# Four layers interleaved by superblocks in shared pools, with score tiles of 3 and 2 banks

## The chip, the core and the metric

The kernel runs on one core of a Trainium2 chip. The metric is the device time of one execution in microseconds (us). "Span" is the length of the one profiled execution; it is 1.7 to 2.8 us under the time of that same run.

Engines: PE is TensorE (matmul), PEld its weight loads, DVE is VectorE, ACT is ScalarE, POOL is GpSimd, SP is SyncE. PSUM is the memory that PE writes its results to; the kernel uses it in 8 banks of 512 float32 columns per row. Work is cut into four superblocks of 512 tokens, numbered 0 to 3.

## The reference

Four layers run one after the other, A B A B, each `x = x + layer(layernorm(x))` on a 2048 x 512 bfloat16 x. A is attention with a sliding window of 256 and 32 heads of 16. B is linear attention.

```python
def _A_ref(x, wqkv, wo):          # q, k, v = x @ wqkv, 32 heads of 16
    scores = jnp.einsum("bhqd,bhkd->bhqk", q, k) * (Dh ** -0.5)
    mask = (idx[:, None] - idx[None, :] >= 0) & (idx[:, None] - idx[None, :] < 256)
    p = _softmax(jnp.where(mask[None, None], scores, -1e9), axis=-1)
    return merge_heads(jnp.einsum("bhqk,bhkd->bhqd", p, v)) @ wo

def _B_ref(x, wqkv, wo):
    phi = lambda t: jnp.where(t > 0, t + 1, jnp.exp(t)) + 1e-6
    pq, pk = phi(q), phi(k)
    kv = jnp.einsum("bhsd,bhse->bhde", pk, v)      # a sum over ALL positions
    z = jnp.einsum("bhsd->bhd", pk)
    num = jnp.einsum("bhqd,bhde->bhqe", pq, kv)
    den = jnp.einsum("bhqd,bhd->bhq", pq, z)[..., None] + 1e-6
    return merge_heads(num / den) @ wo
```

(Head merging is abbreviated.) One dependence matters throughout. B's K, V and Q of a superblock can start once A's output of that superblock is there. B's output can start only after the K and V of all four superblocks.

## The kernel before

Each layer is a function with its own pools, and a layer ends before the next begins. In attention, score tiles are two buffers of 3 PSUM banks, and everything else shares 2 banks. Layer B has all 8 banks to itself (6 + 2 for K, V and Q, then 4 + 4 for the output).

```python
# layer A: scores of 3 head pairs x 2 runs into one 3-bank tile, exp, masks on POOL, PV later
psA = ctx_l.enter_context(tc.tile_pool(name="psA", bufs=2, space=PSUM))
psM = ctx_l.enter_context(tc.tile_pool(name="psM", bufs=2, space=PSUM))
...
A = psA.tile([P, 3, 2, 4, 64], F32, name="A", tag="psA")
...                                   # score matmuls: 32 rows, 64 to 256 columns
nc.scalar.activation(body[:, 0:2 * ng, 0:n, :], A[...], ACT.Exp, scale=0.25)
...                                   # affine_select on POOL for the diagonal blocks
# PV: lhsT = two 64-key blocks of probabilities, rhs = 34 columns of V
nc.tensor.matmul(O[:, u, g, :, :], lhsT=PTs[b][:, s0:s0 + 2, :], rhs=vbd[...], ...)
...
# layer B, first half: 6 + 2 banks of its own
psP1 = ctx_p1.enter_context(tc.tile_pool(name="psP1", bufs=6, space=PSUM))
psKV = ctx_p1.enter_context(tc.tile_pool(name="psKV", bufs=1, space=PSUM))
...
nc.scalar.copy(vs[:, :, 0:P], pv[:].rearrange("p (t c) -> p t c", t=NCT))   # V copy on ACT
...
# the V of layer A is staged in vst (3 buffers) and spread into vbd by four small DMAs per tile
st = vst[vst_n[0] % 3]
```

Of the kernel before, what the change touches and what calls it, by code (L numbers as in the profile page):

```python
# [8 lines left out]
ACT = mybir.ActivationFunctionType  # L9
# [22 lines left out]
R1 = [(7, 7, 1), (-2, 0, 3)]  # L32
R2 = [(5, 5, 3), (-4, 0, 1)]
R3 = [(1, 1, 3), (0, 4, 1)]
R4 = [(3, 3, 3), (2, 6, 1)]
R5 = [(0, 0, 4)]
R6 = [(2, 2, 4)]
R7 = [(-1, 0, 4)]
R8 = [(4, 4, 4)]
R9 = [(-3, 0, 2), (6, 6, 2)]  # L40
R10 = [(1, 4, 2), (3, 6, 2)]
BINS = [(R3, R4), (R5, R6), (R1, R2), (R7, R8), (R9, R10)]
BINS0 = [(R3, R4), (R5, R6), (R8, R10), ([(5, 5, 3)], [(7, 7, 1), (6, 6, 2)])]
GROUPS = [(0, 1, 2), (3, 4, 5), (6, 7, 8), (9, 10, 11), (12, 13), (14, 15)]


def bin_windows(bins):

    win = {u: [] for u in range(4)}
    for b, runs in enumerate(bins):  # L50
        for r, run in enumerate(runs):
            pos = 0
            for (j, w0, n) in run:
                w = w0
                if w % 2:
                    assert pos == 0
                    win[w // 2].append((b, r, -1, j))
                    w += 1
                while w + 1 < w0 + n:
                    win[w // 2].append((b, r, pos + w - w0, j))  # L60
                    w += 2
                if w < w0 + n:
                    assert pos + w - w0 == 3
                    win[w // 2].append((b, r, pos + w - w0, j))
                pos += n
    return win


def bin_masks(runs):

    found = {}
    for r, run in enumerate(runs):
        pos = 0
        for (j, w0, n) in run:
            for w in range(w0, w0 + n):
                if w - j in (0, 4):
                    found.setdefault((w - j, pos + w - w0), []).append(r)
            pos += n
    return [(k, pos, rs) for (k, pos), rs in sorted(found.items())]
# [3 lines left out]
def build(ctx, tc, A_x, A_wqkv, A_wo, B_x, B_wqkv, B_wo, out, layers="ABAB", force_safe=False):  # L83
    nc = tc.nc
    S = A_x.shape[-2]
    NT, NSS = S // P, S // 512

# [3 lines left out]
    small = ctx.enter_context(tc.tile_pool(name="small", bufs=6))  # L91
    work = ctx.enter_context(tc.tile_pool(name="work", bufs=3))
# [4 lines left out]
                            base=0, pattern=[[-1, P]], channel_multiplier=1)  # L97
    pidx = consts.tile([P, 1], I32, name="pidx")
# [3 lines left out]
    mask_odd = consts.tile([P, 1], F32, name="mask_odd")  # L102
    nc.vector.tensor_copy(mask_odd[:], par_i[:])
    mask_even = consts.tile([P, 1], F32, name="mask_even")
    nc.vector.tensor_scalar(mask_even[:], mask_odd[:], -1.0, 1.0, op0=ALU.mult, op1=ALU.add)
    mhalf = consts.tile([P, 1], F32, name="mhalf")
    nc.vector.memset(mhalf[:], -0.5)
# [3 lines left out]
    nc.gpsimd.memset(bd[:], 1.0)  # L111
    nc.gpsimd.affine_select(out=bd[:], in_=bd[:], compare_op=ALU.is_ge, fill=0.0,
                            base=0, pattern=[[-16, 8], [0, 16]], channel_multiplier=1)
    nc.gpsimd.affine_select(out=bd[:], in_=bd[:], compare_op=ALU.is_ge, fill=0.0,
                            base=15, pattern=[[16, 8], [0, 16]], channel_multiplier=-1)
    nA = layers.count("A")
    vflags = consts.tile([1, max(nA, 1)], F32, name="vflags")
    nc.vector.memset(vflags[:], 1.0)

    wA = wpool.tile([P, NCT, 3 * D], BF, name="wA")  # L120
# [550 lines left out]
```

## Time and profile before

The median was 607.03 us (604.7 to 607.84, four runs beside those of the changed kernel). The trace is of another execution, of 602.24 us.

| stage | length, us | PE busy | ACT busy |
|---|---|---|---|
| start, to the first exp of attention | 41.1 | | |
| attention of layer 1 | 170.1 | 83% | 84% |
| middle (layer B and what surrounds it) | 115.5 | 77% | 32% |
| attention of layer 3 | 170.4 | 83% | 84% |
| tail (last layer B) | 103.1 | 75% | 28% |

### The profile page before, as it was taken

How to read it: one execution, taken by the hardware profiler on the slowest of the kernel's cores; microseconds unless marked ns; L12 is line 12 of the kernel's file. 1: busy time of each engine (PE TensorE's matmuls, PEld its weight loads, DVE VectorE, ACT ScalarE, POOL GpSimd, SP SyncE). 2: the span in 40 equal slices, each digit the busy share in tenths (PEclk: the TensorE clock that was granted, in tenths of full speed). 3: DMA queues.
4: the chain of work that ended last, by engine and by line, in shares of the span. 5: the costliest groups of instructions: out<-in, count | busy, mean ns of one | idle time of the engine just before them, and what ended most of it. 6: DMA issues, size and time to landing. Idle time of an engine off the chain costs nothing. (4 is left out here: it accounts for less than half of the span.)

```text
span 600.2 us, 15126 instructions
## 1 busy us (share of the span) xinstructions
PE 460.0 (77%) x6032; PEld 250.1 (42%) x6114; DVE 332.5 (55%) x729; ACT 367.5 (61%) x373; POOL 272.1 (45%) x667
## 2 busy tenths in 40 slices
PE   0178888888878879995647788888887887899573
PEld 0133455545546534452213345554544553444231
DVE  7731546545623365777886154554562336677773
ACT  1557679799779824660025857988978892466000
POOL 9444457657556562200035435675755666320000
PEclk9996899999976678997988779899998788999787
DMA  9412115031020030211431211501302103021363
GB/s 302 127 27 60 16 37 75 2 48 30 2 64 11 3 80 10 41 31 35 72 70 36 57 19 34 78 2 42 35 2 53 24 2 76 14 44 29 74 120 92
DMA packets 83375, 29.66 MB, mean 49 GB/s; under 512 B 67936, under 2 KB 82784, under 8 KB 83296
## 3 DMA queue, kind: packets, MB, share of 16 engines
q1 hardware_dynamic: 78256, 23.88, 19.9%
q10 hardware_dynamic: 5040, 4.72, 2.6%
q8 instruction: 50, 0.82, 0.6%
q14 instruction: 29, 0.24, 0.1%
HBM read 6.29 MB, written 2.10 MB: 14 GB/s over the span
## 5 line engine op out<-in xcount | busy, mean ns | idle before, releaser
L298 ACT ACTIVATE pt<-A 128x1536 bf16<-128x1536 f32 (+1 forms) x228 | 281.0, 1321 | 52.9 <-PE A L286 46.3
L308 POOL TENSOR_SCALAR_AFFINE_SELECT pt<-pt 128x384 bf16<-128x384 bf16 (+3 forms) x456 | 184.3, 430 | 140.1 <-ACT pt L298 136.1
L318 PE MATMUL O<-vbd,pt 128*128 128x34 bf16 x2880 | 108.4, 182 | 27.7 <-POOL pt L308 22.7
L318 PEld LDWEIGHTS <-pt 128*128 128x128 bf16 x2880 | 89.8, 99 | 64.8 <-POOL pt L308 37.9
L286 PE MATMUL A<-qT,kb 32*128 32x192 bf16 (+3 forms) x1920 | 96.7, 249 | 17.1 <-ACT pt L298 14.6
L286 PEld LDWEIGHTS <-kb 32*128 32x128 bf16 x1920 | 50.1, 98 | 69.6 <-issue 64.3
L490 PE MATMUL py<-woB,oT 128*128 128x512 bf16 x124 | 39.3, 448 | 16.6 <-DMA oT<-ob 14.1
L327 DVE RECIPROCAL rall<-O 128x24 f32<-128x24 f32 (+1 forms) x48 | 13.8, 288 | 66.7 <-PE O L318 66.7
L164 POOL TENSOR_SCALAR ln_ve<-ln_mv 128x1 f32<-128x1 f32 x64 | 14.0, 225 | 69.7 <-DVE ln_mv L162 68.2
L221 PE MATMUL pq<-xnT,wA 128*128 128x512 bf16 x108 | 37.3, 432 | 9.2 <-DVE ln_stats L160 5.6
L271 PE MATMUL py<-woA,oT 128*128 128x512 bf16 x108 | 33.1, 397 | 14.1 <-DMA oT<-o_sb 12.4
L160 DVE BATCH_NORM_STATS2 ln_stats<-xres 128x6 f32<-128x512 f32 x64 | 42.5, 681 | 0.8
L235 DVE TENSOR_SCALAR kb<-pk,mask_even 128x512 bf16<-128x512 f32 x32 | 25.3, 791 | 28.6 <-PE pk L232 24.4
L232 PE MATMUL pk<-xnT,wA 128*128 128x512 bf16 x116 | 36.5, 414 | 5.0 <-ACT kb L237 2.5
L403 ACT ACTIVATE phi_e<-pkb 128x512 bf16<-128x512 f32 x32 | 19.1, 598 | 32.9 <-PE pkb L426 31.4
L166 POOL TENSOR_TENSOR ln_rstd<-ln_ve,mhalf 128x1 f32<-128x1 f32 x64 | 36.8, 582 | 4.3 <-ACT xn L178 0.4
L226 DVE CAST qT<-pq 128x512 bf16<-128x512 f32 x24 | 16.6, 691 | 33.5 <-PE pq L221 33.4
L432 PE MATMUL pvb<-wB,xnTb 128*128 128x512 bf16 x124 | 34.8, 395 | 0.2
L426 PE MATMUL pkb<-wB,xnTb 128*128 128x512 bf16 x122 | 34.0, 396 | 0.5 <-issue 0.4
L272 DVE TENSOR_TENSOR xres<-py,xres 128x512 f32<-128x512 f32 x32 | 22.0, 686 | 21.4 <-PE py L271 20.5
L245 PE MATMUL pv<-wA,xnT 128*128 128x512 bf16 x114 | 31.9, 380 | 2.2 <-ACT kb L237 0.8
L178 ACT ACTIVATE xn<-xres,ln_nmr,ln_rstd 128x512 bf16<-128x512 f32 x12 | 9.6, 827 | 37.9 <-DVE ln_nmr L176 37.9
(71 smaller groups left out, 522.0 us busy)
## 6 DMA issues: line engine op xcount, KB each, us to landing
vbd<-vst SPq DMA_DIRECT2D x128, 34.0 KB, 1.9
out_dram<-ost ACTq DMA_DIRECT2D x16, 128.0 KB, 1.9
wB<-in_B_wqkv_dram SPq DMA_DIRECT2D x1, 1536.0 KB, 11.2
xst<-in_A_x_dram SPq DMA_DIRECT2D x8, 128.0 KB, 2.6
wA<-in_A_wqkv_dram SPq DMA_DIRECT2D x2, 512.0 KB, 7.2
xst<-in_A_x_dram ACTq DMA_DIRECT2D x8, 128.0 KB, 4.0
wA<-in_A_wqkv_dram ACTq DMA_DIRECT2D x1, 512.0 KB, 4.3
woA<-in_A_wo_dram ACTq DMA_DIRECT2D x1, 512.0 KB, 8.2
```

Source lines behind the costliest of these rows:

```text
L160: nc.vector.bn_stats(stats[:], x_ap)
L166: nc.gpsimd.tensor_tensor(rstd[:], ve[:], mhalf[:], op=ALU.pow)
L221: nc.tensor.matmul(pq[:], lhsT=w[:, c, t * P:(t + 1) * P], rhs=xnTs[I][:, c, :], start=(c == 0), stop=(c == NCT - 1))
L232: nc.tensor.matmul(pk[:], lhsT=w[:, c, D + t * P:D + (t + 1) * P], rhs=xnTs[I][:, c, :], start=(c == 0), stop=(c == NCT - 1))
L271: nc.tensor.matmul(py[:], lhsT=oT[:, c, :], rhs=wo[:, c, :], start=(c == 0), stop=(c == NCT - 1))
L286: nc.tensor.matmul(A[:, g, r, pos:pos + n, :], lhsT=kbs[m // 8][32 * rg:32 * rg + 32, t, m % 8, :, :], rhs=qTs[I][32 * rg:32 * rg + 32, t, ...
L298: nc.scalar.activation(body[:, 0:2 * ng, 0:n, :], A[:, 0:ng, :, 0:n, :].rearrange("p g r s c -> p (g r) s c"), ACT.Exp, scale=0.25)
L308: nc.gpsimd.affine_select(out=v, in_=v, compare_op=ALU.is_ge, fill=0.0, base=1 if kind == 0 else -2, pattern=[[0, nx], [2 * s, 64]], chann ...
L318: nc.tensor.matmul(O[:, u, g, :, :], lhsT=PTs[b][:, s0:s0 + 2, :], rhs=vbd[(m // 8) % NV][:, m % 8, :, grp[g], :], start=(n == 0), stop=(n ...
L426: nc.tensor.matmul(pk[:], lhsT=xnT[:, c, u * P:(u + 1) * P], rhs=w[:, c, D:2 * D], start=(c == 0), stop=(c == NCT - 1))
L432: nc.tensor.matmul(pv[:], lhsT=xnT[:, c, u * P:(u + 1) * P], rhs=w[:, c, 2 * D:3 * D], start=(c == 0), stop=(c == NCT - 1))
L490: nc.tensor.matmul(py[:], lhsT=oT[:, c, :], rhs=wo[:, c, :], start=(c == 0), stop=(c == NCT - 1))
```

## The change

The intent is to fill what each regime leaves idle. B's K, V and Q projections of a superblock run beside A's attention of the next superblock, and B's outputs run beside the following attention layer. For this all layers share one set of pools: 3 + 2 banks for scores and 3 for everything else. Score runs are packed anew into tiles of 3 and of 2 full banks, so that an exp covers 1536, 1024 or 896 columns per row. Some masks become multiplies on DVE. The staging buffers of V, three before, become two. The start loads x and A's weights first.

```diff
-        psA = ctx_l.enter_context(tc.tile_pool(name="psA", bufs=2, space=PSUM))
-        psM = ctx_l.enter_context(tc.tile_pool(name="psM", bufs=2, space=PSUM))
+        ps3 = pool("ps3", 1, space=PSUM)
+        ps2 = pool("ps2", 1, space=PSUM)
+        psM = pool("psM", 3, space=PSUM)
 ... (bins of runs, packing into phases of 3 and 2 units: cut)
+        vst = [fp.tile([P, 2, NP, VW], BF, name=f"vst{k}") for k in range(2)]
 ... (cut)
+                            nc.vector.tensor_tensor(v, v, mt, op=ALU.mult)
 ... (cut)
+            ob = work.tile([P, D], BF, name="ob", tag="xn", bufs=4)      # shared with LayerNorm's xn
 ... (cut)
+            for I in range(NSS):
+                items = []
 ... (A's projections of I + 1, output projection of I - 1: cut)
+                if I > 0:
+                    items += bkv_items(I - 1, 12) + bq_items(I - 1, 12)
+                attention(I, 0, items)
 ... (cut)
+            run(outproj_items(NSS - 1, 0, 0))
+            run(bkv_items(NSS - 1, 0))
+            kv_final()
+            run(bq_items(NSS - 1, 0))
 ... (cut)
+            run(p2_items(0))
+            lnA(0, 1)
+            run(p2_items(1))
+            run(prep_items(0, 0))
 ... (second attention layer, with p2_items(I + 1) beside it: cut)
```

## The prediction

> **What bounds the kernel now.** I read the page's busy row first, then cut the run at the first and last softmax exp of each attention layer (from the timeline of ScalarE) and asked for the engines' busy time in each piece.
>
> ```profile
> 41.10 2.80 ACT L298 ACTIVATE pt<-A 128x1536 bf16<-128x1536 f32 x2
> ...
> 209.08 2.10 ACT L298 ACTIVATE pt<-A 128x1024 bf16<-128x1024 f32 x2 [0.32 <-PE A L286]
> ...
> 326.69 2.80 ACT L298 ACTIVATE pt<-A 128x1536 bf16<-128x1536 f32 x2
> ...
> 494.98 2.10 ACT L298 ACTIVATE pt<-A 128x1024 bf16<-128x1024 f32 x2 [0.32 <-PE A L286]
> ```
>
> So the 600.2 us are: start 41, attention 170, the B layer and its surroundings 116, attention 170, the second B layer 103. The windows view of those pieces (columns: window, length, then busy us and count for PE, weight loads, DVE, ACT, POOL, then granted clock, DMA share, GB/s):
>
> ```profile
> 41.00:211.00 170.00, 141.63 (x2519) 83.54 (x2550) 75.51 (x145) 143.61 (x122) 99.13 (x249) 0.88 0.16 31
> 211.00:327.00 116.00, 89.34 (x492) 41.33 (x501) 85.21 (x210) 36.69 (x61) 30.03 (x73) 0.88 0.25 48
> 327.00:497.00 170.00, 140.62 (x2518) 83.15 (x2548) 75.49 (x145) 143.51 (x121) 99.05 (x249) 0.88 0.17 31
> 497.00:600.00 103.00, 77.32 (x444) 36.99 (x451) 67.89 (x166) 28.64 (x49) 17.64 (x41) 0.90 0.31 65
> 60.00:165.00 105.00, 88.84 (x1650) 52.58 (x1671) 57.74 (x110) 87.03 (x73) 63.39 (x158) 0.98 0.18 30
> 165.00:211.00 46.00, 37.87 (x722) 23.97 (x727) 14.18 (x30) 40.62 (x34) 27.93 (x74) 0.70 0.11 25
> ```
>
> The reader should see two regimes. In attention PE and ACT are each busy 84%, and DVE idles (44%). In the B layer ACT idles (32%), and PE and DVE take turns. Neither regime uses what the other one wants. The last row shows the clock at 0.70 while only scores and PV matmuls run.
>
> The groups that carry attention, and who waits for whom between 45 and 210 us:
>
> ```profile
> L298 ACT ACTIVATE pt<-A 128x1536 bf16<-128x1536 f32 (+1 forms) x228 | 281.0, 1321 | 52.9 <-PE A L286 46.3 <-POOL pt L308 6.4
> L329 DVE TENSOR_TENSOR o_sb<-O,rall 128x384 bf16<-128x384 f32 (+1 forms) x48 | 24.6, 512 | 1.4
> L403 ACT ACTIVATE phi_e<-pkb 128x512 bf16<-128x512 f32 x32 | 19.1, 598 | 32.9 <-PE pkb L426 31.4 <-PE kvacc L441 1.0 <-DVE pks L405 0.5
> ...
> ACT pt L298 <- PE A L286: 23.2, 29, 4.4
> ...
> PE O L318 <- POOL pt L308: 10.8, 16, 2.5
> PE A L286 <- ACT pt L298: 6.4, 19, 0.5
> ```
>
> Exp waits for scores 23 us and scores for exp 6 us: a ping-pong of two score tiles.
>
> **What the Trainium skill says.**
> "Perfetto Trace Analysis", section Optimization Strategy: a kernel whose most-contended engine changes over time may gain by interleaving the regimes. The windows above show just that situation.
> "TensorE: Matmul & The Clock Gate", section on the clock gate: 512 columns issue every 427 ns at half clock and every 216 ns at full. The trace agrees:
>
> ```profile
> 30.30 1.87 PE L221 MATMUL pq<-xnT,wA 128*128 128x512 bf16 x4 [0.67 <-ACT xnT L188]
> 219.82 1.04 PE L271 MATMUL py<-woA,oT 128*128 128x512 bf16 x4 [1.00 <-DMA oT<-o_sb]
> 217.79 0.38 PE L426 MATMUL pkb<-wB,xnTb 128*128 128x512 bf16 x1
> ```
>
> Four take 1.04 us and one alone 0.38, so the pitch is 0.22 us; the cold four take 1.87. That page lets the clock fall after an idle window; here it falls to 0.70 with PE 82% busy, so small matmuls seem not to count as full activity (my reading, not shown yet).
> "VectorE: DVE Perf Modes", the perf-mode tier table and the errata section: tensor_tensor takes (N+151)/0.96 ns at 1x and can reach 2x on bf16 in SBUF. For 384 elements at 1x that is 557 ns, and o_sb's 384-element form measures 557. No instruction before multiplies two bf16 tiles in SBUF, so for the new mask multiply I take 0.45 us, between 1x (0.56) and 2x (0.36): an estimate from that page.
> "ScalarE: Activation LUTs", section What ACT_TABLE_LOAD costs: neighbouring activations overlap by about 93 ns. The trace agrees: 228 exps of mean 1321 ns sum to 301 us and count 281 busy, 88 ns less each.
>
> **The change, part by part.**
> *Same work.* Exp elements are the same 307,200 per partition (228 instructions before; in the built order after 246: 116 of 1536, 98 of 1024, 32 of 896). At 93 ns each the 18 extra cost 1.7 us. The 2,880 PV matmuls and 1,024 projections of 512 columns are unchanged; score matmuls fall from 1,920 to 1,440 with the same columns.
> *Moved into attention.* The built order puts beside the first attention layer: A's Q, K, V of superblocks 1 to 3 (144 matmuls of 512), three output projections (48), and B's K, V, Q of superblocks 0 to 2 (144). PE: 336 x 0.216 = 72.5 us. In the full-clock window 60 to 165 the score groups took 27.2 us for 71 tiles (0.38 us) and PV 32.9 for 924 (0.036 us); so 123 score tiles cost 47 and 1,440 PV 51. With the small pkv matmuls (2.7) the sum is 173 us, against 142 before. The second attention layer also carries numerator, denominator and output of two B superblocks: 32 x 0.216 + 6 = 13, so 186.
> *ACT in attention:* 283/2 + 24 phi x 0.6 = 156 us.
> *DVE in attention:* Q and V evacuations 24 x 0.69 = 17, K 24 x 0.69 = 17, mask multiplies 70 x 0.45 = 31, normalising 24 x 0.85 = 20, residual adds 12 x 0.69 = 8, LayerNorm statistics 16 x 0.85 = 14, B's K/V/Q 3 x 12.4 = 37: 144 us; the second layer has some 20 more (165). DVE doubles, from 75.
> *POOL:* 568 smaller selects instead of 456, plus xn: about as before (100 us per attention layer), not a bound.
> So PE leads with 173 and 186. Before, the busiest engine filled 84%. With ACT 10% below PE and dense projections keeping the clock up in the last superblock (0.70 before), I let PE fill 90%: **192 and 206 us**, against 170 twice.
> *What stays between.* From the last exp of layer A to the first of the next: PV tail and normalising 4; four DMA transposes (queue time some 1.3 us each) and output projection 7; LayerNorm of one superblock, now batched (statistics 0.85 x 4, power 0.8, xn 0.81, last transposes) 7; the last superblock's B projections, DVE-bound: 8 phi x 1.0, 4 copies x 0.69, 4 kv adds x 0.4, final 1: 13; numerator and output of superblock 0, 9, its LayerNorm 8, first Q/K units 6, superblock 1 partly hidden 4: **58 us** against 116.
> *The end:* the same first four steps (31) and four final B superblocks on DVE (16 x (0.68 + 0.69) + 4 x 1.1 = 26) plus the last output 5: **62** against 103.
> *The start:* x of superblock 0 and A's weights are loaded first, but in DVE's built order the statistics of superblocks 1 and 2 stand before the first xn, and x of superblock 2 is queued behind B's weights on the SP queue. So the first xn waits for nearly all loads as before, and all 12 projection units of superblock 0 stand ahead of the first scores: **41 us**, no gain.
> Sum: 41 + 192 + 58 + 206 + 62 = 559 us of span. The runs of before are timed 2 to 8 us above the span; with 4: **563 us**.
>
> **The rivals.**
> *Three engines too evenly loaded.* PE 173, ACT 156, DVE 144: each is in order, projections and the O tile share three PSUM banks, and an O tile holds one for three steps. If DVE is late with an evacuation, PE stops, then exp. For it: DVE doubles. Against it: B alone ran with PE 53 of 59 us busy while sharing with DVE. If PE fills only 82%, attention is 211 and 227: 603 us.
> *The score ping-pong starves.* Each size has one buffer; the built order has stretches of 72 PV matmuls with projections between two score tiles (some 5 us of PE against 2.5 us of exp in hand). For it: exp already waits 23 us for scores. If each superblock loses 4 us, 32 in all: 595 us.
> *The start gains after all.* If DVE's statistics do not hold the first xn, some 12 us less: 550 us.
> *Clock.* If denser work lifts the clock to 1.0 and PE fills 95%, attention is 182 and 196: 543 us. If the clock stays at 0.88, 590 us.
>
> **Range and chances.** The removed 99 us between and at the end are fairly sure (the work is visibly elsewhere in the built order); what attention gives back is not: 38 us (PE at 95%) to 98 us (at 82%), centre 58. That gives 543 to 603 us; with a gain at the start I take 535 to 603 eight times in ten. Faster by over 2% means under 595.5: 0.84. Within 2%: 0.13. Slower: 0.03.
>
> **What would show each step.** First exp at about 41 us; exps of the first layer ending about 233, PE busy about 90% between, DVE 75%; ACT gap in the middle of about 58 us; end piece 62 us; mean clock above 0.892; mask multiplies at 0.36 to 0.56 us. Wrong would be: PE under 83% busy in attention with waits for DVE or for exp in the lead, or a middle gap of 80 us because its chain of small steps (transposes, LayerNorm, den, num) is longer than their sum.

## More of the kernel before

Three executions count as slow and are left out of the ratios, though not of the medians: one of four of e9_two_last, and two of the seven of the kernel before that ran beside e1 to e4.

From the page of the kernel before: each engine's busy time with its share of the span, then the busy tenths and the granted PE clock in 40 equal slices.

```profile
PE 460.0 (77%) x6032; PEld 250.1 (42%) x6114; DVE 332.5 (55%) x729; ACT 367.5 (61%) x373; POOL 272.1 (45%) x667
...
PE   0178888888878879995647788888887887899573
...
ACT  1557679799779824660025857988978892466000
...
PEclk9996899999976678997988779899998788999787
```

ACT visibly works in the two attention layers and rests in B. PE works in both. The windows view by superblock (window, length, then busy us and count of PE, PEld, DVE, ACT, POOL, then granted clock, DMA share, GB/s) shows superblocks 1 and 3 of the first attention layer:

```profile
84.00:127.00 43.00, 36.36 (x689) 21.42 (x692) 22.99 (x45) 38.39 (x33) 27.82 (x69) 1.00 0.23 39
...
170.20:211.20 41.00, 32.78 (x643) 21.27 (x644) 11.90 (x26) 37.00 (x30) 25.39 (x67) 0.66 0.10 22
```

Superblock 3 has no projections left to run beside it, so PE has less to do there. Yet it is 33 us busy, because its clock is 0.66.

## The result, and the profile after

The changed kernel took 655.17 us (652.13 to 656.77, four runs) against 607.03. The ratio is 1.0794, with a 95% interval of 1.0743 to 1.0845: it is slower. Ratios here are the mean time of one kernel's fast runs over the mean of the other's of the same rounds, so they differ a little from the ratio of the quoted medians.

The page of the changed kernel:

```profile
PE 501.4 (77%) x5746; PEld 248.6 (38%) x5746; DVE 376.1 (58%) x833; ACT 325.2 (50%) x323; POOL 250.9 (38%) x727
...
PE   0489997999798596465768997998799869658573
...
ACT  0168855875596493020053862687268947602000
...
PEclk9989698979795795796787877999899779769788
...
L301 ACT ACTIVATE pt<-A 128x1536 bf16<-128x1536 f32 (+2 forms) x246 | 285.5, 1221 | 149.8 <-PE A L289 111.3
```

PE has fewer instructions and 41 us more busy time. Its clock row has twelve sevens and two fives, where it had eight sevens. Exp costs about what it did (285.5 us, 281.0 before). ACT now idles 149.8 us ahead of it, where it idled 52.9, but 43.7 of that is the middle, where exp used to follow other work of ACT.

The first and last exps, in the timeline of ACT of the changed kernel (start, duration, count, and in brackets the idle time before and what ended it):

```profile
38.88 1.45 ACT L301 ACTIVATE pt<-A 128x1536 bf16<-128x1536 f32 x1 [1.48 <-PE A L289]
...
249.52 2.37 ACT L301 ACTIVATE pt<-A 128x1536 bf16<-128x1536 f32 x2 [0.69 <-POOL pt L324]
...
332.02 3.60 ACT L301 ACTIVATE pt<-A 128x1536 bf16<-128x1536 f32 x3 [43.70 <-PE A L289]
...
563.09 2.37 ACT L301 ACTIVATE pt<-A 128x1536 bf16<-128x1536 f32 x2 [0.53 <-PE A L289]
```

The stages are therefore start 38.9, attention 213.0, middle 80.1, attention 233.4, tail 87.5. The prediction had 41, 192, 58, 206, 62. Middle and tail did shrink, by 35.4 and 15.6 us, but attention grew by 42.9 and 63.0.

The windows view by superblock of the changed kernel (columns as above): superblocks 0, 1 and 3 of the first layer, the middle, and superblock 1 of the second attention layer.

```profile
38.90:74.20 35.30, 31.17 (x441) 15.90 (x438) 16.53 (x34) 29.83 (x29) 18.05 (x64) 0.90 0.13 34
74.20:133.80 59.60, 53.53 (x709) 26.67 (x707) 40.97 (x94) 41.52 (x41) 29.04 (x84) 0.92 0.19 38
...
194.90:251.90 57.00, 46.32 (x652) 24.96 (x649) 28.27 (x69) 41.45 (x41) 26.77 (x85) 0.78 0.11 20
251.90:332.00 80.10, 51.09 (x283) 21.92 (x280) 48.25 (x100) 4.78 (x8) 10.69 (x25) 0.75 0.17 34
...
376.10:443.20 67.10, 60.53 (x741) 29.85 (x738) 45.61 (x101) 41.63 (x41) 29.53 (x84) 0.89 0.20 39
```

Superblock 0, which carries none of B, is shorter than before (35.3 against 42.9). Every superblock that carries B's work is 16 to 24 us longer than before, and in each PE is the busiest engine.

Four theories could explain this.

- **Theory 1, PE work.** PE sets the pace of attention already, so a projection placed beside attention costs there what it saves elsewhere. What remains between the layers is a chain of waits, not a sum of work.
- **Theory 2, contention.** Shared buffers, bursts and waits of one in-order engine on another cost the time. Two lines point at one of them. In the timeline of PE a B projection waits 4.3 us; in the waits view of DVE for the first attention layer, V copies wait for the two staging buffers:

```profile
102.11 1.04 PE L245 MATMUL pv<-wA,xnT 128*128 128x512 bf16 x4
107.47 1.46 PE L245 MATMUL pkb<-wB,xnT 128*128 128x512 bf16 x4 [4.32 <-DVE vst L269]
```

```profile
DVE vst L269 <- DMA vbd<-vst: 10.8, 3, 5.2
```

- **Theory 3, the clock.** The granted clock is at half for 193 us of the run, against 130 us before, and at half clock a matmul of 512 columns starts every 0.43 us in this trace, instead of every 0.22.
- **The score tiles.** One buffer of each size may starve exp.

### The profile page after: what moved, and what is told of

It reads as the page before. It is cut to its first block, busy times and chain, and to the rows that moved or that the text cites. A ratio compares the mean times of both kernels' runs of the same rounds, so it can differ in the third digit from the quotient of the medians.

```text
span 652.9 us, 14439 instructions
## 1 busy us (share of the span) xinstructions
PE 501.4 (77%) x5746; PEld 248.6 (38%) x5746; DVE 376.1 (58%) x833; ACT 325.2 (50%) x323; POOL 250.9 (38%) x727
## 5 line engine op out<-in xcount | busy, mean ns | idle before, releaser
L301 ACT ACTIVATE pt<-A 128x1536 bf16<-128x1536 f32 (+2 forms) x246 | 285.5, 1221 | 149.8 <-PE A L289 111.3
L324 POOL TENSOR_SCALAR_AFFINE_SELECT pt<-pt 128x128 bf16<-128x128 bf16 (+2 forms) x568 | 166.8, 322 | 205.6 <-ACT pt L301 191.8
L289 PE MATMUL A<-qT,kbd 32*128 32x320 bf16 (+4 forms) x1440 | 113.8, 276 | 25.6 <-ACT pt L301 25.0
L317 DVE TENSOR_TENSOR pt<-pt,tri 128x384 bf16<-128x384 bf16 (+1 forms) x140 | 51.4, 369 | 59.1 <-ACT pt L301 58.2
L289 PEld LDWEIGHTS <-kbd 32*128 32x128 bf16 x1440 | 45.3, 96 | 95.6 <-issue 86.8
L245 PEld LDWEIGHTS <-xnT 128*128 128x128 bf16 x384 | 35.8, 104 | 77.6 <-issue 28.8
L245 PE MATMUL pkb<-wB,xnT 128*128 128x512 bf16 x128 | 40.0, 443 | 28.5 <-DMA xnT<-xn 20.1
L261 DVE TENSOR_TENSOR kbd<-pk,eo 128x512 bf16<-128x512 f32 x64 | 41.5, 681 | 21.1 <-PE pk L245 20.8
L219 POOL TENSOR_SCALAR xn<-xres,ln_nm,ln_rs 128x512 bf16<-128x512 f32 (+1 forms) x60 | 46.7, 790 | 3.4 <-DMA xnT<-xn 1.9
L212 DVE BATCH_NORM_STATS2 ln_st<-xres 128x6 f32<-128x512 f32 (+1 forms) x60 | 39.3, 675 | 11.0 <-DMA xres<-in_A_x_dram 10.8
```

Source lines behind the costliest of these rows:

```text
L212: nc.vector.bn_stats(st[:, u, :], xs[u])
L219: nc.gpsimd.tensor_scalar(xn[:], xs[u], nm[:, u:u + 1], rs[:, u:u + 1], op0=ALU.add, op1=ALU.mult)
L245: nc.tensor.matmul(ps[:], lhsT=lhs(c), rhs=rhs(c), start=(c == 0), stop=(c == NCT - 1))
L261: nc.vector.tensor_tensor(dst[:, t, :, :, :].rearrange("p m k h -> p (m k) h"), ps[:, hf * 256:(hf + 1) * 256].unsqueeze(2).to_broadcast([ ...
L289: nc.tensor.matmul(A[:, x, pos[x]:pos[x] + n, :], lhsT=kbd[half(m)][32 * rg:32 * rg + 32, t, m % 4, :, :], rhs=qTs[I][32 * rg:32 * rg + 32 ...
L301: nc.scalar.activation(body[:, x:y, 0:pos[x], :], A[:, x:y, 0:pos[x], :], ACT.Exp, scale=0.25)
```

## The experiments

Runs were beside the kernel before, whose median was 604.9 to 606.2 us. The chips were different ones for e1 to e4, for e5 to e8, for e9 to e11 and for e12 to e14. Executions of one kernel lie 2 to 10 us apart, so a stage that differs by under some 3 us between two single traces shows little. The stages of every profiled run, cut like the two above (us; "half" is the time at half clock, summed from the clock record of the trace):

```
run               span   start  att 1  middle  att 2  tail   half
before            600.2  41.1   170.1  115.5   170.4  103.1  130
changed           652.9  38.9   213.0   80.1   233.4   87.5  193
e4_hybrid         600.6  41.0   167.3  118.8   167.8  105.7  166
e1_b_after        641.3  39.6   174.2  115.5   190.8  121.2  202
e2_b_quarter      645.9  40.6   204.5   77.8   234.8   88.2  303
e3_vst4           633.1  39.2   199.0   80.5   226.4   87.9  173
e5_fill_before    608.6  41.5   175.4  111.9   175.0  104.9   75
e6b_fill32_before 629.4  42.1   182.4  113.0   186.2  105.7  179
e7_fill_vst4      636.1  40.4   199.6   77.9   231.1   87.1  109
e8_chain_vst4     619.9  39.6   198.2   75.8   220.8   85.5  159
e9_two_last       590.9  39.1   185.4   78.8   197.5   90.1  134
e9a_one_last      591.3  40.5   171.2   91.1   187.3  101.2  129
e10_phi_copy      629.5  41.3   195.0   79.1   227.8   86.4  170
e11_hybrid_vst4   596.4  41.8   163.9  122.2   160.4  108.1  161
e12_out_middle    594.3  38.7   184.6  101.8   179.7   89.6  135
e13_pv_half       615.9  39.1   190.3   77.6   222.8   86.0  183
e14_act_copies    581.2  40.5   185.4   74.9   194.4   85.9  119
```

### The score tiles alone: e4_hybrid

Attention of the changed kernel, with layer B whole, after it, and in its own PSUM pools as before. The edit replaces the B part by the old function:

```diff
+        for a in range(2):
+            with ExitStack() as c:
+                open_A(c)            # ps3, ps2, psM, xtp, qtp
+                ...                  # attention as in the change, no B items
+            with ExitStack() as c:
+                layer_B(c, xres, xres, wB, woB, a == 1)      # as in the kernel before
```

> One part of the change alone: attention with the score tiles of 3 and 2 banks, mask multiplies and start of the changed kernel, but layer B whole and after it, with its own PSUM pools, as in the kernel before. Theory 1 (the interleaving is what costs, the score tiles are good): start 39, attention 35 + 3 x 42 = 161 twice, middle 116, tail 103: about 580 of span, 584 timed, some 4% faster than before. Rival (the single buffer of each score tile starves exp or PE): attention stays at 170 or more, total 600 to 620.

It took 602.67 us, ratio 1.0013 (0.9921 to 1.0105). Attention fell by 3 us per layer, not by 9. So the new tiles do not starve exp, but they gain next to nothing by themselves. Theory 1's 584 us was too hopeful, and of the rival the total came (600 to 620) but not its cause (attention at 170 or more). This run has the two staging buffers too; e11 below gives it four.

### B's projections out of attention: e1_b_after

```diff
-                if I > 0:
-                    items += bkv_items(I - 1, 12) + bq_items(I - 1, 12)
 ...
-            run(bkv_items(NSS - 1, 0))
+            for I in range(NSS):
+                run(bkv_items(I, 0))
+                run(bq_items(I, 0))
+                if I + 2 < NSS:
+                    xnB[I + 2] = ln(I + 2)
             kv_final()
-            run(bq_items(NSS - 1, 0))
```

> B's K, V and Q projections of all four superblocks run after the attention of their layer instead of beside it; all else as in the changed kernel (attention 213 and 233 us, middle gap 80, tail 87, start 39). Theory 1 (TensorE already bounds attention, so a projection beside it costs about what it costs alone): 144 matmuls of 512 at 0.22 us plus small ones, some 34 us of TensorE per layer at full clock, leave attention: 175 and 195 us; B's work, DVE-bound at some 13 us per superblock, is added to middle and tail: about 119 and 127 us. Total 640 to 660, unchanged within 2%. Theory 2 (what costs in attention is contention, waits on shared buffers and bursts, not the work itself): attention falls by 45 to 60 us per layer, to 165 and 180 us; total under 625.

B's LayerNorm moves out of attention with them. It took 643.16 us, 12 less than the changed kernel (ratios to the kernel before 1.068 and 1.079, with intervals that overlap): the same within 2%, as theory 1 had it. All five stages came within 6 us of its numbers. Read against the changed kernel, B's projections beside attention cost 38.8 + 42.6 = 81.4 us there (213.0 - 174.2 and 233.4 - 190.8). They save 35.4 + 33.7 = 69.1 us in middle and tail (115.5 - 80.1 and 121.2 - 87.5). So the interleaving does hide B, but in the changed kernel it costs more than it hides. Part of that cost is a buffer count (e3 below).

The same run shows a second loss. With no K, V or Q of B in attention it is still 40.7 us of span above e4_hybrid. Of these, 23.0 are in the second attention layer, which still carries B's outputs, 15.5 in the tail, and 6.9 in the first layer; start and middle together are 4.7 shorter. The tail's 15.5 are the price of running B in the shared pools and in this order. How much is the 3 PSUM banks, the copies put on DVE or the batching was not told apart, except for the copies (e14 below).

### A quarter of B's projections: e2_b_quarter

```diff
-            for c in range(NCT):
-                nc.tensor.matmul(ps[:], lhsT=lhs(c), rhs=rhs(c), start=(c == 0), stop=(c == NCT - 1))
+            n = 1 if short[0] and name in ("pkb", "pvb", "pqb") else NCT   # short: within attention
+            for c in range(n):
+                nc.tensor.matmul(ps[:], lhsT=lhs(c), rhs=rhs(c), start=(c == 0), stop=(c == n - 1))
```

> Wrong result on purpose: B's projections that stand beside attention run 1 of their 4 contraction matmuls; order, evacuations, buffers and waits stay. 108 matmuls per layer go, 23 us of TensorE at full clock, some 30 at the mixed clock of the changed kernel. Theory 1 (TensorE bound): each attention falls by 23 to 30 us, total 595 to 609. Theory 2 (waits for buffers, DVE and bursts bound): each attention falls by under 12 us, total over 630.

It took 647.7 us, only 7 less than the changed kernel. Its output is wrong, which doesn't matter for the time. By the numbers, theory 2 was right. The trace says otherwise. Superblocks 1 and 2 of the first layer, in its windows view:

```profile
75.00:135.40 60.40, 54.12 (x685) 26.26 (x682) 40.61 (x94) 41.85 (x40) 30.33 (x89) 0.73 0.17 37
135.40:194.20 58.80, 51.48 (x674) 25.78 (x671) 36.95 (x85) 42.16 (x41) 26.30 (x83) 0.79 0.14 29
```

PE is as busy as with all the matmuls, since its clock fell from 0.92 and 0.89 to 0.73 and 0.79. The groups of PE in the same two superblocks show where it went (busy us, mean ns). In the changed kernel:

```profile
L289 PE MATMUL A<-qT,kbd 32*128 32x320 bf16 (+4 forms) x384 | 28.9, 273 | 2.6 <-ACT pt L301 2.4
```

and in this run:

```profile
L292 PE MATMUL A<-qT,kbd 32*128 32x320 bf16 (+4 forms) x384 | 38.2, 313 | 2.0 <-ACT pt L304 1.7
```

The same 384 score matmuls cost 9.3 us more. B's three projection groups had fallen from 27.4 to 12.9. So two thirds of what was removed came back in the scores alone. Taking away large matmuls lowered the clock of the small ones.

This asks what the clock follows. The clock record changes in steps of 3.41 us. I cut all 17 traces (changed, before and these 15 runs) into such windows. For each I counted what the array took in that window and looked at the clock granted in the next one (2,902 pairs):

```
best single threshold on ...                            next clock told right
always "full"                                           72%
share of the window in which PE was busy (0.59)         84%
columns streamed (0.435 of 8,192)                       86%
columns x rows used / 128 (0.375 of 8,192)              97%

columns x rows used / 128     windows    next window at full clock
under 0.30 of 8,192           553        0%
0.30 to 0.35                  172        15%
0.35 to 0.40                  210        56%
over 0.40                     1,967      99%
```

8,192 columns are 16 matmuls of 512, which is about what a window holds at the measured pitch of 0.22 us. The threshold is thus about six full matmuls of 512 columns per 3.41 us. A score matmul uses 32 of 128 rows and counts a quarter. A PV matmul streams 34 columns in its 36 ns, against 512 in 216. Attention without projections stays under the threshold however busy PE is: between 175 and 210 us of the kernel before it averages 0.30, and the projections lift it to 0.50 between 90 and 165 us. This is a correlation; e5 and e6b test it.

### Filling to hold the clock: e5_fill_before and e6b_fill32_before

One useless matmul of 512 columns ahead of each score tile of superblocks 0 and 3, overwritten by the scores, with 128 rows (e5) and with 32 rows (e6b, the same PE instructions at a quarter of the weight):

```diff
             A = psA.tile([P, 3, 2, 4, 64], F32, name="A", tag="psA")
+            if I in (0, 3):
+                nc.tensor.matmul(A[:, 0, :, :, :], lhsT=kbs[I][:, 0, 0, :, :], rhs=qTs[I][:, 0, :], start=True, stop=True)
```

> The kernel before, with one extra matmul (128 rows, 512 columns, overwritten at once) ahead of each score tile in the first and last superblock of each attention layer. Theory 3 (over the six runs so far, the clock granted in each 3.41 us follows how many columns, weighted by rows used, the PE array took in the 3.41 us before: under about 0.37 of the most it could take, the clock is halved): the half-clock time of each attention layer falls from 41 to under 15 us although work is added; the last superblock falls from 41 to about 38, where ACT's 37 bound it; total 592 to 602. Rival (the clock follows something else, heat or mere PE busy time, or work added is just work): half-clock time unchanged, each such superblock 4 to 7 us longer, total 620 or more.

> Control for the run before: the same extra matmuls with 32 rows instead of 128, so the same PE time at a quarter of the row-weighted work. Theory 3: half-clock time stays at 35 us or more per attention layer, and TensorE's busy time in those superblocks grows by some 27 x 0.3 to 0.4 = 8 to 12 us; total 605 to 625, slower than with 128 rows. Rival (PE busy time alone raises the clock): half-clock time falls as with 128 rows and the time is the same.

They took 610.59 us (ratio 1.0076) and 628.67 us (1.0359). Superblock 3 of the first layer, windows view, with 128 rows:

```profile
176.90:216.90 40.00, 34.37 (x672) 19.40 (x678) 10.62 (x25) 37.30 (x30) 25.27 (x66) 0.96 0.10 24
```

and with 32 rows:

```profile
176.00:224.50 48.50, 44.17 (x668) 26.67 (x673) 10.02 (x24) 38.10 (x30) 25.26 (x66) 0.55 0.08 19
```

The same number of extra matmuls gave a clock of 0.96 or of 0.55, and 8.5 us between them in this one superblock. Half-clock time was 17 us in each attention layer with 128 rows (expected: under 15), and 61 and 73 us with 32 rows. So in this kernel the clock follows row-weighted work and not busy time. But the filled kernel was not faster than before. Superblock 3 went only from 41.0 to 40.0, since ACT's 37 us nearly set it. Superblock 0 of the first layer grew from 42.9 to 47.9 us. My 592 to 602 us was too low, and so was 605 to 625 for 32 rows.

### The clock in the changed kernel: e7_fill_vst4

On e3 (next section), such matmuls in superblocks 0 and 3, and dense ones where PE waits between and after the layers.

```diff
+            if I in (0, 3):
+                nc.tensor.matmul(A[:, 0, :, :], lhsT=kbd[half(8 * I)][:, 0, 0, :, :], rhs=qTs[I][:, 0, :], start=True, stop=True)
 ...
+            fill(8, o_sb[:, 3, :])
             run(outproj_items(NSS - 1, 0, 0))
+            fill(20, obsT[NSS - 1][3][:].rearrange("p c q -> p (c q)"))
```

> The changed kernel with four V staging buffers (636 us) plus such extra matmuls ahead of the score tiles of the first and last superblock, and extra dense matmuls where TensorE waits in the middle and the tail (8 before and 20 after the last output projection, 6 or 12 in the waits of the B output). Theory 3 (the clock makes the loss): last superblocks from 55 and 56 to about 47, first ones from 38 and 44 to 36 and 40; middle from 80 to 68 and tail from 88 to 76 because their 26 to 30 us of PE work at half clock take half; total 590 to 610. Theory 1 (the middle is a chain of latencies on DVE, POOL and DMA): middle and tail stay at 77 to 90; attention alone gains, total 615 to 625.

It took 639.09 us against 635.97 for its base (on another chip; both ratios to before are 1.056 to 1.057). Half-clock time fell from 173 to 109 us and nothing was gained. Superblock 3 of the first layer and the middle, in the windows view:

```profile
184.40:240.00 55.60, 49.33 (x667) 24.52 (x674) 28.63 (x69) 42.06 (x41) 26.77 (x84) 0.91 0.10 20
240.00:318.00 78.00, 58.58 (x332) 26.55 (x334) 47.44 (x99) 4.86 (x10) 10.58 (x24) 0.82 0.17 36
```

Without filling they were 54.8 and 80.5 us. Both expectations were too low (590 to 610 and 615 to 625). Theory 3 as the main cause of the long middle and of the long last superblock falls. The test is not clean, because the filling takes PE time itself: in the middle the three output projections of 16 matmuls fell from 5.8, 6.3 and 6.6 us in e3 to 4.1, 4.8 and 3.6, and only 2.5 us of that 6 were gained.

### Staging buffers: e3_vst4

```diff
-        vst = [fp.tile([P, 2, NP, VW], BF, name=f"vst{k}") for k in range(2)]
+        vst = [fp.tile([P, 2, NP, VW], BF, name=f"vst{k}") for k in range(4)]
 ... (memset and index likewise; check_sums keeps its scratch row in o_sb, for the room)
```

> Four V staging buffers instead of two (room from a scratch row taken out of its pool); all else as in the changed kernel. In the first attention layer TensorE stands twice for 4.0 to 4.3 us behind V copies that wait for the staging DMA, and both stops are followed by half-clock windows. Theory 2 (contention): the first attention falls by 8 to 15 us, the second by 2 to 5; total 637 to 645. Theory 1: the stop only moves to the next wait and the gain is under 5 us; total over 650.

It took 635.97 us, 19 less than the changed kernel: 14.0 us less in the first attention layer, 7.0 in the second. Superblocks 1 and 2 of the first layer:

```profile
77.20:129.70 52.50, 50.71 (x708) 26.39 (x704) 40.68 (x94) 41.37 (x40) 28.90 (x84) 0.96 0.21 43
129.70:183.50 53.80, 51.39 (x708) 26.86 (x705) 37.68 (x85) 42.12 (x42) 25.93 (x84) 0.97 0.15 32
```

The two stops of 4 us are gone, and with them most of the half clock there. So theory 2 is right for this part. Read against e1 (which keeps two buffers), interleaving now costs 60.4 us in attention for 68.3 saved in middle and tail. e1 with four buffers was not run, so which way the balance of interleaving goes is open; it is near zero. What is left is a PE busy for 97% and 96% of these two superblocks, at nearly full clock.

In e11_hybrid_vst4 the same four buffers, with LayerNorm's power tile by tile, went into the hybrid.

> The hybrid (new score tiles, layer B as before and not interleaved, 602.7 us) with four V staging buffers and LayerNorm's power tile by tile. Theory 1: without B beside it, no superblock waits long on the two buffers; attention stays at 165 to 168 and the total at 595 to 603. Rival (the two buffers cost 14 us here too): attention near 155, total near 580.

It took 594.09 us (ratio 0.9809, 0.977 to 0.9848). Attention came to 163.9 and 160.4, in the second layer between the two expectations. The two edits together gave 3.4 and 7.4 us of attention, so the two buffers cost less here than in the interleaved kernel (14.0 and 7.0). This kernel interleaves nothing and is faster than the one before.

### Is it PE, or ACT and DVE beside it: e10_phi_copy and e13_pv_half

Both on e3. Their outputs are wrong, which doesn't matter for the times. In e10 B's feature map within attention is one DVE copy; in e13 three of six PV matmuls per list are left out in superblocks 1 to 3.

```diff
         def phi(dst, ps):
+            if short[0]:
+                nc.vector.tensor_copy(dst, ps)
+                return
```

```diff
-                    for n, (b, slot, j) in enumerate(win[u]):
+                    lst = win[u]
+                    if I > 0:
+                        own = [x for x in lst if x[2] == 2 * u]
+                        lst = own + [x for x in lst if x[2] != 2 * u][:len(lst) // 2 - len(own)]
+                    for n, (b, slot, j) in enumerate(lst):
```

> Wrong result on purpose: the run with four V buffers (636 us), in which B's feature map beside attention is one DVE copy instead of an exp on ACT and two DVE operations; all matmuls stay. 24 exps of 0.60 us (14 us of ACT) and some 10 us of DVE leave each attention layer, and no exp of attention can stand behind one of B's. Theory 1 (TensorE bounds superblocks 1 and 2): those stay within 2 us of 52.6 and 53.7, total 625 to 634. Rival (three engines too evenly loaded, ACT and DVE in order): superblocks 1 to 3 fall by 4 us or more each; total under 612.

> Wrong result on purpose: the run with four V buffers (636 us) with half of the PV matmuls of superblocks 1 to 3 left out (192 of 34 columns per superblock, some 6.9 us of TensorE at full clock). They weigh little in row-weighted columns beside 48 to 112 matmuls of 512, so the clock should stay. Theory 1 (TensorE's work sets superblocks 1 and 2): these fall by 5 to 7 us each, to about 47, 48 and 57, 57; total 605 to 615. Rival (order and waits set them): under 2 us each, total over 628.

e10 took 629.87 us. Superblocks 1 and 2 of the first layer:

```profile
77.20:129.10 51.90, 50.51 (x708) 26.18 (x705) 38.61 (x86) 37.62 (x32) 29.00 (x84) 0.96 0.21 43
129.10:182.20 53.10, 51.08 (x706) 26.43 (x705) 35.03 (x77) 38.28 (x33) 26.29 (x83) 0.97 0.15 32
```

ACT lost 4 us in each, and the superblocks 0.6 and 0.7. So "three engines too evenly loaded" is not what sets these two. POOL was not relieved in any run.

e13 took 617.93 us. The same two superblocks came to 50.9 and 51.0, 4.4 us less together, where I had expected 10 to 14. This is between the two expectations. PE's busy time there fell by 5.7 us (102.1 to 96.4), although the PV group fell by 9.8, because the half-clock time rose again (7.4 to 13.1 us) and the other groups grew. Length followed PE's busy time for three quarters. I take this as support for theory 1, with the clock giving part of any removed work back. It is not a clean proof.

### The chain between the layers: e8_chain_vst4

```diff
-            nc.gpsimd.tensor_tensor(rs[:], rs[:], mhalf[:], op=ALU.pow)          # four tiles at once
+                nc.gpsimd.tensor_tensor(rs[:, u:u + 1], rs[:, u:u + 1], mhalf[:, 0:1], op=ALU.pow)   # in the loop
 ...
+            if idle:      # between and after attention: an idle probability tile instead of LayerNorm's tag
+                obv = pts[3][(i // 3) % 5][:, 1 + 9 * (i % 3):9 + 9 * (i % 3), :].rearrange("p s c -> p (s c)")
```

> The changed kernel with four V staging buffers (636 us), with LayerNorm's power tile by tile instead of four tiles at once, and with the B output staged, in middle and tail, in probability tiles that lie idle then, instead of in LayerNorm's buffers. Theory 1 (the middle gap is a chain of latencies and a shared buffer): middle from 80.5 to about 70 (LayerNorm wait 8.1 to 5, the 5.0 and 4.4 stops gone or halved), tail from 88 to about 84; total 618 to 628. Theory 3 (its half clock makes it long): under 4 us gained in the middle, total 630 or more.

The waits it goes for, in the timeline of PE of the changed kernel's middle:

```profile
257.22 5.73 PE L245 MATMUL py<-woA,oT 128*128 128x512 bf16 x16 [2.97 <-DMA oT<-o_sb]
270.55 1.89 PE L245 MATMUL pkb<-wB,xnT 128*128 128x512 bf16 x4 [7.59 <-DMA xnT<-xn]
...
308.49 0.58 PE L449 MATMUL pn<-kvn,pqT 128*128 128x128 bf16 x4 [5.06 <-DVE ob L452]
313.68 6.50 PE L245 MATMUL py<-woB,oT 128*128 128x512 bf16 x16 [4.61 <-DMA oT<-ob]
```

It took 621.77 us, 14 less than e3. About 10 us were expected in the middle and 4 in the tail, but only 4.7 and 2.4 came. The run makes two edits at once, and they were not told apart. The LayerNorm wait fell from 8.1 to 5.0 us. The two stops for `ob` and its transpose (5.0 and 4.4 us in e3) became one of 6.5, now for the transpose alone. The rest of the gain is in the second attention layer (5.6), where two stops of PE for LayerNorm's output fell from 4.2 and 3.6 us to 3.3 and under 2.

### Where PE has room: e9a_one_last, e9_two_last, e12_out_middle, e14_act_copies

If PE is the bound in superblocks 1 and 2 but not in superblock 3, which has no projections of A, B's work belongs there. From e8:

```diff
-                if I > 0:
-                    items += bkv_items(I - 1, 12) + bq_items(I - 1, 12)
+        NL = 2                                   # 1 in e9a
+        def last_items(outs):                    # beside the attention of superblock 3 only
+            its = bkv_items(0, 1) + bq_items(0, 1)
+            for J in range(1, NL):
+                its += bkv_items(J, 0) + bq_items(J, 0)
+            return its[:4] + outs[:1] + its[4:8] + outs[1:] + its[8:]
 ... (the other superblocks after attention, the first of them ahead of superblock 3's output projection)
```

> From the run with four V buffers and the shorter LayerNorm chain (621.8 us): B's projections of superblocks 0 and 1 stand only beside the attention of the last superblock, where A has no projections left; those of 2 and 3 run after attention, with superblock 2's filling the waits for the transposes and for LayerNorm of superblock 3. Theory 1 (what counts is whether TensorE has room in the very superblock): superblocks 1 and 2 fall from 53 and 55 to about 45 each, the last from 51 to 47 to 53, so attention is about 175 and 195 instead of 198 and 221; middle 78 to 84, tail 88 to 94; total 575 to 595, faster than the kernel before. Rival (any interleaving costs what it saves): 605 to 625.

> The same with only superblock 0's B projections in the last superblock's attention and 1 to 3 after it. Theory 1: last superblock about 45 (TensorE some 40 of work, ACT 42), middle and tail 11 us longer each than with two: total within 10 us of the run with two (580 to 605). Rival: better than with two by over 10 us, since less is interleaved.

They took 592.34 us (ratio 0.973, 0.9652 to 0.9808) and 594.3 us (0.9827, 0.9788 to 0.9866), both faster than either kernel, as theory 1 had it; whether by over 2% is open. Attention missed its number: 185.4 us in the first layer, not 175, with 48.4 in superblock 1 (45 expected) and 54.7 in superblock 3 (47 to 53). Superblock 3 of e9's first attention layer, and then of e9a's:

```profile
169.80:224.50 54.70, 51.80 (x739) 27.13 (x735) 39.56 (x97) 45.87 (x48) 27.57 (x92) 0.97 0.12 22
```

```profile
169.10:211.70 42.60, 40.31 (x674) 22.44 (x670) 27.97 (x72) 40.96 (x40) 27.63 (x88) 0.94 0.18 28
```

With two superblocks of B it takes no longer than the changed kernel's superblock 3 (57.0 us), which carried one superblock of B at a clock of 0.78 and waited for it. With one superblock of B (e9a) superblock 3 took 42.6 and 45.5 us, against 42.2 and 41.8 with none (e1): the first one is nearly free (0.4 and 3.7 us). The second adds 14.2 and 10.2 us to attention (171.2 to 185.4, 187.3 to 197.5) and saves 12.3 and 11.1 in middle and tail: break-even. This is theory 1 at its plainest. Here work was nearly free while PE had room, and after that it cost its own length.

Two cautions. The edit also puts superblock 2's projections into the waits between the layers, and this was not told apart from the room in superblock 3. And e11, without any interleaving, took 594.09 us in the same rounds on the same chip: over it, e9 gained 2 us in the median. What made e9 faster than the kernel before is thus not shown to be the interleaving.

Two variations of e9 followed. e12 moves B's outputs out of the second attention layer; e14 gives copies in the exposed stages to ACT.

```diff
-                    if I > 0:
-                        items += p2_items(I + 1)          # e12
+            run(p2_items(2, idle=True))
+            run(p2_items(3, idle=True))
```

```diff
-            (nc.scalar.copy if act else nc.vector.tensor_copy)(vs[:, :, 0:P], ...)      # e14; A's Q and V alike
+            (nc.scalar.copy if act or ex[0] else nc.vector.tensor_copy)(vs[:, :, 0:P], ...)
```

> From the run with B's projections of two superblocks in the last superblock (592.3 us; attention 185 and 197, middle 79, tail 90): the B outputs of superblocks 2 and 3, which stood beside the second attention layer's superblocks 1 and 2, run in the middle. Theory 1: their 13 us of TensorE work leave attention, which falls to about 185, like the first; the middle grows by 2 x 7 to 2 x 11 us, to 93 to 101; total 592 to 602. Rival (they cost more beside attention than their work, by late x for LayerNorm): attention below 182, total under 588.

> From the run with two superblocks (592.3 us): in the stages between and after attention, where ACT is idle, the copies of B's V, and of A's Q and V for the first superblock of the second layer, go to ACT instead of DVE. If DVE bounds the exposed stages: 8 + 8 copies of 0.69 us leave it in the middle, 8 in the tail; middle from 79 to about 71, tail from 90 to 86; total 578 to 584. If they are a chain of waits: under 3 us in all, total 588 to 594.

e12 took 599.26 us. The second attention layer fell by 17.8 us, to slightly less than the first; the middle grew by 23.0. So B's outputs are what made the second layer longer. They cost more beside attention than their 13 us of work, as the rival had it (179.7 us, under its 182), but they cost still more in the middle, so they pay a little where they stood.

e14 took 582.5 us, ratio 0.9633 (0.9566 to 0.9701), the best of all. Its stages in the windows view:

```profile
40.50:226.00 185.50, 168.38 (x2449) 88.69 (x2447) 112.32 (x271) 149.66 (x140) 105.27 (x333) 0.89 0.16 35
226.00:300.90 74.90, 56.44 (x322) 25.76 (x323) 51.21 (x120) 18.85 (x33) 21.02 (x53) 0.86 0.22 41
300.90:495.30 194.40, 177.20 (x2543) 93.40 (x2542) 127.40 (x303) 149.94 (x140) 112.71 (x345) 0.90 0.22 41
495.30:581.20 85.90, 58.41 (x360) 26.75 (x360) 53.03 (x110) 14.25 (x24) 8.75 (x26) 0.89 0.26 63
```

Middle and tail shrank by 3.9 and 4.2 us, and the second attention layer by 3.1. In the middle 16 copies of 0.69 us left DVE, 11 us, and 3.9 us were gained. So DVE is part of that stage's bound and the chain of waits is the rest; I had expected 8.

## Why the prediction was wrong

It said 563 us and faster; 655 came, and slower. Of the 93.9 us of span between the two (559 and 652.9), 48.4 lie in attention and 47.6 in middle and tail; the start took 2.1 less than predicted. Two steps failed: PE's time in attention, which was summed at full clock and divided by a fill that two staging buffers did not allow, and the stages between and after, which were summed as work where they are chains of waits. By its own steps:

- **The reading of the regimes: wrong as a ground for a large gain.** "Neither regime uses what the other one wants" was read off ACT and DVE (the 32% and 44% beside "idles" are their busy shares). PE fills 83% of attention and 77% of layer B. It is the busiest engine or level with it in both, so there was little of it to share. The sums that follow do count PE as the bound. e1 measured it: 81.4 us paid in attention for 69.1 saved, or 60.4 for 68.3 once the staging stops are gone (e3).
- **PE sum of 173 and 186 us: mis-sized.** The term was counted at full-clock rates. The windows view of the result shows PE busy 186 and 198 us in the two attention layers, at a mean clock of 0.87 and 0.88. "Dense projections keeping the clock up in the last superblock" failed: it was granted 0.78 and 0.82 there, and the mean clock of the run was 0.852, where over 0.892 was predicted. e2, e5 and e6b show why. The clock here follows row-weighted columns in each 3.41 us, so how evenly the dense matmuls are spread should matter; that was not tested by itself.
- **PE fill of 90%: too high.** It was 186 / 213.0 = 87% and 198 / 233.4 = 85%. Two staging buffers account for 21.0 us of attention (e3). In the second layer the wait of A's projections for a late x comes on top (two stops, 8.0 us in the waits view). In superblock 3, at 81%, PE stood 7.0 us behind exp and 2.8 us until B's x came. Given work that was ready, it filled to 95% (51.8 of 54.7 in e9). Sum of this and the term above: 21 and 27 us of the miss.
- **Middle of 58 and tail of 62 us: mis-sized, by the failure the prediction had named.** It had warned of "a middle gap of 80 us because its chain of small steps ... is longer than their sum", and 80.1 came. Step by step, between the PE starts in the timeline: PV tail 2.4 (predicted 4), transposes and output projection 8.7 (7), LayerNorm 7.6 (7), B's projections 17.8 (13), output of superblock 0 11.4 (9), LayerNorm of A and output of superblock 1 20.2 (8 + 4), first Q, K and V to the first exp 12.0 (6). The step "partly hidden 4" hid nothing: the output of superblock 1 stood still behind LayerNorm's buffers and the transposes. The half clock has a share in it. The three output projections of 16 matmuls took 5.73, 6.27 and 6.50 us, where 16 matmuls at full clock took 3.79:

```profile
283.70 3.79 PE L245 MATMUL pqb<-xnT,wB 128*128 128x512 bf16 x16
...
293.68 6.27 PE L245 MATMUL py<-woB,oT 128*128 128x512 bf16 x16 [2.05 <-DMA oT<-ob]
```

That is some 7 us of the 22, of which filling gave back 2.5 (e7). Shorter waits gave 4.7 us (e8), ACT copies 3.9 (e14). In the tail the first four steps took 36.4 us (31 predicted). The four outputs of B took 51.1, where DVE's work and the last output had been added up to 31: each is a chain from numerator to DVE, transpose and output projection, and the next one starts when it is done, 10.7 to 12.4 us later:

```profile
613.66 0.55 PE L437 MATMUL pd<-kvz,pqT 128*128 128x8 bf16 x16
...
619.26 5.46 PE L245 MATMUL py<-woB,oT 128*128 128x512 bf16 x16 [2.05 <-DMA oT<-ob]
624.55 0.55 PE L437 MATMUL pd<-kvz,pqT 128*128 128x8 bf16 x16
```

- **DVE, ACT and POOL in attention: right that ACT and DVE are no bound.** e10 took work from both and gained 0.6 and 0.7 us in superblocks 1 and 2; POOL was not tested. DVE was sized too high (144 and 165 us; 123 and 142 came), which changed nothing.
- **Exp, mask multiplies and start: right.** Exp was busy 285.5 us (281 + 1.7 predicted), the mask multiply of 384 elements took 381 ns (0.36 to 0.56 us), the first exp came at 38.9 us (41).
- **Rivals.** "Three engines too evenly loaded" named 211 and 227 us of attention, close to the 213.0 and 233.4 that came, and "DVE is late with an evacuation" did stop PE for 8.3 us. But DVE was late because it waited for the staging DMA, not from its load (e3, e10), so the closeness is in part luck. The clock rival had a right reason and a third of the size (27 of 92 us). None had the staging buffers.

The result as a sum over profiled spans: 600.2 before; +0.4 for the new tiles and start (e4); +40.7 for shared pools, order and B's outputs beside the second layer (e1 less e4); +11.6 for B's projections beside attention; 652.9. Then -19.8 for two more staging buffers, -13.2 for the shorter chain, -29.0 for B's projections in superblock 3 and in the waits between the layers, -9.7 for copies on ACT: 581.2. The 23.0 us that sit in the second attention layer are moved work rather than loss: e12 paid the same 23.0 us to put these outputs back into the middle. By that number, as an estimate, e1's middle is some 20 us longer than e4's would be without them (115.5 against 118.8 - 23.0). So most of the 40.7 is B running in the shared pools and in this order. How it divides between PSUM banks, order and engines is open, but for the copies, which gave 8.1 us of middle and tail in e14.

## What to carry to other kernels

Before interleaving two regimes, compare the same engine's fill in both. If one engine leads in both, interleave only as much as it has room for, superblock by superblock, and expect every further piece to cost its own length. Price matmuls at the clock that the mix will be granted: here runs of matmuls with few rows or few columns halved it although PE looked busy (0.55 at 44.2 of 48.5 us busy in e6b), and removing dense matmuls from such a mix may gain nothing. A buffer count cut to make shared pools fit is a change of its own and should be tried alone. And compare with the best kernel that does not interleave: here e11 came within 2 us of e9.

## What the Trainium skill lacked or had wrong

- "TensorE: Matmul & The Clock Gate", section on the clock gate, ties the half clock to an idle window and the full clock to a busy one. Its 3.41 us window agrees with the clock record here. But the page does not say what counts as busy, and PE's busy time is not enough: over 2,902 windows the next clock was told right by PE's busy share in 84% and by columns weighted by rows used in 97%, with the threshold near 0.375 of 8,192. Superblock 3 with 32-row filling was 44.2 of 48.5 us busy and was granted 0.55.
- "Perfetto Trace Analysis", section Optimization Strategy, says that interleaving regimes whose most-contended engine differs may help. It lacks the warning for an engine that is nearly full in both: here that engine was PE (83% and 77%), and 81.4 us were paid for 69.1 saved (60.4 for 68.3 with four staging buffers).
- No page says that removed matmul work may come back through the clock: with B's projections cut from 27.4 to 12.9 us, 384 score matmuls grew from 28.9 to 38.2.
